# Float64 weight blocks assembled on other engines: two integer passes on VectorE instead of three, one more activation on ScalarE, no clamp on GpSimd, and a new instruction order

## The chip, the cores and the metric

One core of a Trainium2 chip runs the kernel. The metric is the device time of one execution in microseconds (us). The kernel before was timed in three runs: median 474.81 us, lowest 474.49, highest 475.64.

## The reference: what is computed

Three stages on batch 2, sequence 768, model width 512 (8 heads of 64):

```
attention:  q, k hashed to 6 sign bits by proj; a key is masked unless all 6 bits agree with the query's;
            softmax(q k^T / 8) v                                  -> x  (2, 768, 512)
experts:    4 experts of width 64: q,k,v = x @ wq[e], wk[e], wv[e]; causal softmax attention, @ wo[e];
            the two best experts by x @ w_gate, weighted by a softmax over their two logits
mix:        xk = mu_k*x + (1-mu_k)*x_prev,  xr likewise
            out = sigmoid(xr @ w_r) * (relu(xk @ w_k)**2 @ w_v)
```

The last three weight matrices, `w_k` (512x1024), `w_r` (512x512) and `w_v` (1024x512), reach the kernel as float64. All products are made with float16 pairs (a high part and the rest), three matmuls for one product, so each weight is needed as a float16 pair.

## The kernel before, in words

The program treats 12 blocks of 128 rows (6 for each batch). Each goes through attention (per head: scores `s`, exponential `P`, float16 pair `PHL`, transposed pair `PT`, product `x`), experts (`qk`, `vg`, `se`, `y`, `o`) and mix (`m32k`, `m32r`, `mk`, `mr`, `h`, `r`, `v`). Blocks overlap: while one is in its attention, earlier ones are in their experts or mix.

The weights are loaded and split once, in the first part of the run. `split_d` treats one 128x512 block of a float64 matrix; it is called 20 times (8 blocks of `w_k`, 4 of `w_r`, 8 of `w_v`). The block comes as pairs of 32-bit words (`raw`: word 1 `top` holds sign, exponent and high mantissa bits, word 0 `low` the rest). A float32 is put together bit by bit:

- ScalarE takes the absolute value of `top`, read as a float32, into `wm` (called `mag` in the code).
- GpSimd clamps `wm` from below and above, in place.
- VectorE, pass 1: shift `wm` left by 3 and mask, into the PSUM tile `wd`. Pass 2: OR in the upper three bits of `low`. Pass 3: OR in the top two bits of `top`.
- ScalarE writes the float16 high part of `wd` (tiles `WK`, `WR`, `WV`), and VectorE the rest ("the rest pass").

Engines named in the profile: PE is TensorE, DVE is VectorE, ACT is ScalarE, POOL is GpSimd, SP issues nearly all DMAs.

Every instruction is recorded first (class `Program`) and then issued in an order that is written out: `ORDER`, a packed list of indices, gives one sequence for all engines, and `HOMES` gives each tile its buffer. Each engine takes its instructions in that sequence. So an instruction that waits holds up all that stand behind it on its engine. All instructions are issued from one line (L200), so the profile tells them apart by tile names. Other passes that the prediction speaks of: `naq`, `nak` and `v` on VectorE (the rest passes of queries, keys and values; each subtracts one tile in SBUF from another tile in SBUF), and on GpSimd the rest pass `PHL<-P,PHL` of every softmax, which reads two tiles in SBUF.

Of the kernel before, what the change touches and what calls it, by code (L numbers as in the profile page):

```python
# [909 lines left out]
AL`%`NekJrE;Pr2xEcy!3(SFQ;11rywNMU|lBY$`5WB-9Ish49G9{yyco5b>D{O>?aWNc%eb5O5{SD<YIUR=17=eyJe!P#>aXL+<wpbVAQb%ZwZLkQYpiVFg  # L910
8sicuic_c}N2HPP6CH)6@BmZNC`d)iU>d!|hd6_l!z=s~X3}i>3*u2noDEH|7|wz9@B!OldyGnR;Wfsmc`%FSLo|AXkMRw5h9}qq7C-`eiwP+ab-+0^kDB5_
I18yMF?GSYG@rWSQ+$ryFgkt2?)VA+rti1`Ho`j`0>@xIJ;NCE8NXmJ?2W(UCU}8SXfyo40XPu1z##00G3gvUwD)+G7EljNPsiaa#-d0x1kb}z9ERWU8Ugjk
p12i|7ScB8gM*Q1KlR0*=>T1)3viHz;~yA@rr-#?2$L`}#U`e+l!25S4TTdRG!;+6IjY1N$><VH#>-HRtMDPZL8ss<ROVqY3e!*$s>*3;1^q|=z<F9kS70oT
!+#+it)vY!8mHlOJWONoH2j4#@D3cOOjMm~@CnLHH)%YM#JM;D&p<7%$=6^bU56Vm5wp-HnvK8lue_DAQcjwKwfR4&!}Bl)&BP;gi#F31I!cS_0v&TpXer%<
yKoEc!F-JBve7K;&)F##<)H<5lD5%8T!c@cE-$0sc{yFA+pvljV{Y0`tLYTohrILvrgC(*1efA6jOmu+eY!(`Vhr~X9zi{h<sQQt+ClZX0Y8PEv;r^DW%`Gr
xqs;yyn&MRC&hNZ&?=1U9#AP-jnjAoo~B*2mex@Px<^;2G?k$>IDpsVK>mw1VjQ;;<GH`_7(Isst}Hd=P52h}Qai3lmFWfSqlE4ywCDJ)95v!fG>F&YI=oA}
X%98$rrels(=a|m@1O-Y<Cgp$rgH~=NL8pRHQ`slID;L|<nmOFPPoBboj$;8$VVTcAU&c_Fpjt2W6Dp3=m`}j!6H<YQs8*rj$3gXeuiQ+frs-`QY=obxFhet
o!FXF;t(!ChP%+?2%g2Wxf6Hh67-C^a!sm5zfui)LC@(W1$;$sXd<V=Hr$PC({3EeqqsZ&MiH<My`@BMGcMqF)P=u5TTbj=(`Y{KhVpyr!GEyl)L553(r5ZY
&FCvd<TMx<xE>*=#c!0v)u*rU6Mv#~IG3kz8CTXZf2Z{LfyQu8p2XkaJ2aqP91$mTN|(VAN8m{8_y_goKAg%mq`o{<gp;}-(2oJLxh6D+Pr7-W+Ld$J-6_|I
# [33 lines left out]
HOMES = """
c-lQwi?-S}5S-c7TdKpQ;4~?v#)Rho|F9#ITmc7;ywc8V0p<$TK*mnji|&~bg!Y=}VsuN5aHz%uh7LGrZraeh;t#k5-0fd}vw!#nfAPuxF#Jz^<=^~ijvp$l
_Jz&9;lqCL%AY9sj>xafB&t_NFMQxb`>48*qeSgzdb4hb34)e{YBc7SvDt1D$a@JXtd?28<m#&@_kCNe-kK0EOqmPSxA4s*4zN^_4!R%7rV72HN`TNC6Edb2
$5I(2NH7;`cAtXuEql9N)c0f`D{jDpy0?0m!ewL*!E|vSNI(~;=n*9}(N2eQ#}YNSDZzoPOiIf&MPAw}?k~je6UCS?hBp~dDpF6hNOdYTzMBP4=&FkLaNTt*
kzuN4O%8gKbK=UoI`fh4H|}jk$C;&bH9n`WJ|s?1929^g-br{$i){TZ^}`;9-%Bc}ac7ws@LU5@kO{6rOV=0dazhg3lksYHIyiK+9?^UtTG2<uvy`<qq)d^t
i~UAVnL@O{QKh~ISLTNCVe;V7&I_NH2XB7!%Uv+I4QWrQ;3^cz_dAxPjE$0^fYEYelVBdKt4uekq>J2OL#t}6Q1mI3?L5xEiFR398|OiJd=)~wo}Mqew8bBG
rL8#4sxHu(Q|}y_Vl)^=bd)q7@aT}R>+~;z`hlRJE8;k!WxSuWS--qA4axTH>6=CoDWgc|(T&wAhN2*`n?f0ptN89G`-CeGtxqGNYq9Ryy081ywtmJ%qMlzD
#Z{6iWi^i@-rYMxEIR2OqsU6hc9PkjSZ%h>l#*5Msr7K?r-HSe^z{_!g?BD-<*uig;T(w}yYP1?W5%8<On19XY0vd@2By=fCCHySJ1%xz<GgH|jAh+VxZblR  # L960
S$jWi%9G%ZfZAkNDw+lTLnu=S^N&hdQd|Y+i1{y-r>`+ir8R95&gCUvo5s8Eud}b))w@0UKMxuncK
"""


# [40 lines left out]
```

## Time and profile before

| | before |
|---|---|
| median of the runs | 474.81 us |
| the profiled execution's own time | 473.49 us |
| its span, first to last instruction | 471.3 us |
| PE, DVE, ACT, POOL busy | 428.7, 354.1, 344.6, 320.8 us |
| mean granted TensorE clock | 0.978 of full speed |

Busy times are sums over the whole span; stages have different limits, so the rows further down are cut by stage. Times in rows are us unless they say ns. In rows of groups the columns are: line, engine, operation, output<-inputs, shapes, count | busy us, mean ns of one | idle time of the engine just before them and what ended it.

### The profile page before, as it was taken

What the parts mean: (1) busy time and instruction counts of PE and PEld (TensorE: products, weight loads), DVE (VectorE), ACT (ScalarE), POOL (GpSimd) and SP (SyncE); (2) the same over time, 40 slices, a digit from 0 to 9 for tenths busy, and PEclk for the clock granted to TensorE, in tenths of its full rate; (3) what the DMA queues carried; (4) which work ended last, traced back from release to release, by engine and by line L of the source; (5) the groups of instructions that cost most, each with busy time, mean ns of one, the idle gap of its engine ahead of it and who ended that gap; (6) DMA issues with size and microseconds to landing.
All of it is one profiled execution on the core that took longest, in us unless ns stands there. A gap on an engine that the chain in (4) does not pass through costs nothing.

```text
span 471.3 us, 15541 instructions
## 1 busy us (share of the span) xinstructions
PE 428.7 (91%) x6296; PEld 326.4 (69%) x6296; DVE 354.1 (75%) x990; ACT 344.6 (73%) x654; POOL 320.8 (68%) x321
## 2 busy tenths in 40 slices
PE   2873788788999999999999999999999999999996
PEld 2752476677667779687668768967857778787563
DVE  4999999999999887999776678675676634643422
ACT  4388897999999896659888987889678867353221
POOL 1878898788887958867888668669667753561010
PEclk9886999989999999999999999999999999999999
...
GB/s 256 273 236 167 196 187 212 152 184 196 188 193 197 155 184 170 170 161 166 188 205 168 159 148 175 171 131 202 166 151 102 169 160 24 113 96 56 76 69 45
DMA packets 227160, 75.59 MB, mean 160 GB/s; under 512 B 218512, under 2 KB 222736, under 8 KB 227088
## 3 DMA queue, kind: packets, MB, share of 16 engines
q1 hardware_dynamic: 225584, 74.48, 85.2%
...
## 4 chain that ended last, share of the span: by engine, by line
PE 59%; DVE 14%; POOL 12%; DMA 6%; issue 5%; ACT 2%; SPq 1%; ACTq 0%; POOLq 0%; DVEq 0%
PE v L200 12%; PE h L200 10%; PE s L200 7%; POOL PHL L200 7%; PE x L200 5%; PE r L200 5%; PE qk L200 5%; DVE P L200 3%; PE se L200 3%; PE y L200 2%; PE o L200 2%; PE vg L200 2%; PE tr_y L200 2%; DMA x<-nbq 2%; DVE wd_v L200 1%
## 5 line engine op out<-in xcount | busy, mean ns | idle before, releaser
L200 POOL TENSOR_TENSOR PHL<-P,PHL 128x768 f16<-128x768 f32 x96 | 158.9, 1666 | 30.6 <-ACT PHL L200 25.6
L200 DVE TENSOR_SCALAR_CACHE_REDUCE P<-s 128x768 f32<-128x768 f32 x96 | 91.1, 952 | 12.3 <-PE s L200 6.0
L200 ACT ACTIVATE P<-P,mx 128x768 f32<-128x768 f32 x96 | 89.0, 929 | 15.2 <-DVE mx L200 11.9
L200 PE MATMUL s<-y,x 128*128 128x384 f16 x384 | 80.5, 339 | 7.6 <-DVE P L200 5.1
L200 PE MATMUL h<-mk,WK 128*128 128x128 f16 x1152 | 74.1, 219 | 0.0
L200 PEld LDWEIGHTS <-WK 128*128 128x128 f16 x1152 | 67.6, 98 | 5.0 <-DVE vn L200 0.3
L200 PE MATMUL x<-v,PT 128*128 128x64 f16 x1728 | 63.4, 194 | 2.0 <-DVE g L200 0.8
L200 PEld LDWEIGHTS <-PT 128*128 128x128 f16 x1728 | 59.3, 99 | 7.8 <-DMA PT<-PHL 2.5
L200 ACT ACTIVATE PHL<-P 128x768 f16<-128x768 f32 x72 | 59.9, 838 | 5.0 <-DMA PT<-PHL 1.9
L200 PEld LDWEIGHTS <-x 128*128 128x128 f16 x576 | 41.2, 99 | 31.3 <-issue 11.1
L200 PE MATMUL v<-WV,k2h 128*128 128x512 f16 x192 | 57.1, 379 | 0.0
L200 POOL TENSOR_TENSOR PHL_m<-P_m,PHL_m 128x512 f16<-128x512 f32 (+2 forms) x24 | 33.8, 1424 | 19.2 <-ACT PHL_m L200 18.8
L200 PE MATMUL qk<-xT,WQK 128*128 128x128 f16 x576 | 37.1, 219 | 0.7 <-DVE xT L200 0.5
L200 PE MATMUL v<-WV,k2l 128*128 128x512 f16 x96 | 36.4, 379 | 0.0
L200 PEld LDWEIGHTS <-WQK 128*128 128x128 f16 x576 | 33.9, 98 | 3.1 <-issue 1.2
L200 PE MATMUL r<-WR,mr 128*128 128x512 f16 x144 | 35.7, 379 | 0.0
L200 DVE SCALAR_TENSOR_TENSOR h<-h,t 128x512 f32<-128x512 f32 x24 | 16.7, 696 | 21.5 <-ACT t L200 21.5
L200 ACT ACTIVATE P_m<-P_m,bias_m 128x512 f32<-128x512 f32 (+2 forms) x24 | 19.7, 820 | 14.0 <-DVE P_m L200 13.5
L200 POOL TENSOR_SCALAR PHL<-P 128x768 f16<-128x768 f32 x24 | 20.5, 853 | 10.7 <-ACT P L200 8.9
L200 ACT ACTIVATE t<-h 128x512 f32<-128x512 f32 x24 | 14.1, 589 | 18.0 <-PE h L200 18.0
L200 POOL TENSOR_TENSOR mk<-m32k,mk 128x512 f16<-128x512 f32 x12 | 13.9, 1158 | 18.2 <-ACT mk L200 18.2
L200 PEld LDWEIGHTS <-k2h 128*128 128x128 f16 x192 | 16.8, 98 | 12.3
(143 smaller groups left out, 877.7 us busy)
## 6 DMA issues: line engine op xcount, KB each, us to landing
...
PT<-PHL SPq DMA_TRANSPOSE x88, 4.3
```

The source lines that it names most:

```text
L200: getattr(getattr(self.nc, engine), method)(*[real(a) for a in args], **{k: real(a) for k, a in kw.items()})
```

## The change

`split_d` puts the float32 together in another way:

```diff
-F64_MIN = float(np.array([0x38100000], np.uint32).view(np.float32)[0])
+REBIAS = 2.0 ** -112
...
-        top, low = raw[:, :, 1], raw[:, :, 0]
-        nc.scalar.activation(mag, top.bitcast(F32), AF.Abs)
-        nc.gpsimd.tensor_scalar(mag, mag, 3e38, F64_MIN, op0=OP.min, op1=OP.max)
+        top = raw[:, :, 1]
+        end = sp.tile([P, n], U32, tag="b2", bufs=NB2, name=f"we_{nm}")
+        nc.scalar.activation(mag, top.bitcast(F32), AF.Abs, scale=REBIAS)
+        nc.scalar.activation(end, raw.bitcast(U8)[:, :, 3], AF.Copy, bias=-15.5 / 32, scale=1.0 / 32)
         w = dps(f"wd_{nm}", [P, n])
         u = w.bitcast(U32)
-        nc.vector.tensor_scalar(u, mag.bitcast(U32), 3, 0x3FFFFFFF, op0=OP.logical_shift_left, op1=OP.bitwise_and)
-        nc.vector.scalar_tensor_tensor(u, low, 29, u, op0=OP.logical_shift_right, op1=OP.bitwise_or)
-        nc.vector.scalar_tensor_tensor(u, top, 0xC0000000, u, op0=OP.bitwise_and, op1=OP.bitwise_or)
+        nc.vector.scalar_tensor_tensor(u, mag.bitcast(U32), 3, end, op0=OP.logical_shift_left, op1=OP.bitwise_or)
+        nc.vector.scalar_tensor_tensor(u, top, 0x80000000, u, op0=OP.bitwise_and, op1=OP.bitwise_or)
...
 ORDER = """
-(2566 entries, packed)
+(2546 entries, packed)
 HOMES = """
-(1291 entries, packed)
+(1311 entries, packed)
```

The absolute value is now multiplied by a power of two, so no mask and no clamp are needed. The upper three bits of `low` are made by ScalarE from the highest byte of `low` (times 1/32, with a bias so that rounding cuts off) into a new SBUF tile `we` (called `end` in the code). VectorE's new pass 1 reads two SBUF tiles, `wm` and `we`, and writes PSUM; its pass 2 puts in the sign.

`ORDER` and `HOMES` are new throughout. Read as instructions, the two orders compare so:

| | before | after |
|---|---|---|
| VectorE instructions | 810 | 790 |
| ScalarE instructions (without DMA issues) | 494 | 514 |
| GpSimd instructions | 317 | 297 |
| TensorE groups, SP's DMAs | 724, 215 | 724, 215 |
| assembling passes of VectorE ahead of `xT` of block 0, 1, 2, 3 in its queue | 21, 31, 42, 55 of 60 | 14, 20, 28, 37 of 40 |
| instructions of VectorE ahead of these | 116, 167, 236, 311 | 111, 156, 220, 296 |
| ScalarE instructions ahead of the last `P` of block 1, 2, 3, 4 | 70, 106, 145, 194 | 74, 115, 161, 210 |
| assembling passes of a block that stand directly behind one another | 2 pairs | 9 pairs |
| changes between exponential and sigmoid on ScalarE, the first included | 16 | 18 |

Among the instructions that both have, many stand elsewhere (by the longest common sequence 435 of TensorE's 724 groups, 441 of VectorE's 750, 96 of SP's 215), mostly by a few places. SP's first DMAs are before: queries, keys, a part of `wv`, and three more of keys; after: queries, the four of keys, then values.

## Rows read from the trace of the kernel before

**Rows 1.** The page: span, and busy time, share and instructions of each engine.
```profile
span 471.3 us, 15541 instructions
...
PE 428.7 (91%) x6296; PEld 326.4 (69%) x6296; DVE 354.1 (75%) x990; ACT 344.6 (73%) x654; POOL 320.8 (68%) x321
```
**Rows 2.** Busy time by stretch, us from the span's start.
```profile
core 0: us, PE busy (x) PEld busy (x) DVE busy (x) ACT busy (x) POOL busy (x), PEclk, DMA share, GB/s
0.00:12.00 12.00, 3.64 (x32) 3.22 (x33) 5.75 (x9) 5.82 (x7) 1.98 (x7) 1.00 0.90 255
12.00:96.00 84.00, 62.88 (x928) 48.06 (x927) 82.39 (x213) 65.13 (x124) 71.45 (x75) 0.90 0.93 203
96.00:160.00 64.00, 58.54 (x923) 46.26 (x919) 62.27 (x182) 61.73 (x122) 54.50 (x55) 0.97 1.02 188
12.00:160.00 148.00, 121.42 (x1845) 94.32 (x1843) 144.66 (x394) 126.86 (x245) 125.95 (x129) 0.93 0.97 196
160.00:460.00 300.00, 296.22 (x4382) 225.44 (x4381) 200.99 (x585) 210.05 (x401) 192.90 (x186) 1.00 0.84 143
460.00:471.30 11.30, 7.43 (x44) 3.43 (x41) 2.68 (x4) 1.82 (x3) 0.00 (x0) 1.00 0.12 46
```
**Rows 3.** The chain of waits, first us 12 to 160, then 160 to the end.
```profile
by line: POOL PHL L200 16.4%; issue 10.5%; DVE P L200 10.5%; PE qk L200 5.2%; DVE wd_v L200 4.4%; DVE wd_k L200 3.7%; DMA w_v<-in_moe_wv_dram 3.5%; PE s L200 3.4%; DVE x L200 3.2%; DVE y L200 2.4%; POOL PHL_m_p L200 2.3%; ACT P L200 2.0%; P
...
by line: PE v L200 17.4%; PE h L200 15.5%; PE s L200 9.3%; PE r L200 8.1%; PE x L200 7.8%; PE qk L200 5.2%; PE se L200 4.1%; PE vg L200 3.4%; PE y L200 3.4%; PE o L200 3.2%; DMA x<-nbq 3.1%; POOL PHL L200 3.0%; issue 2.0%; PE tr_y L200 1.7%
```
**Rows 4.** Timeline of DVE: start, length, operation.
```profile
74.48 0.69 DVE L200 TENSOR_SCALAR wd_r<-wm_r 128x512 uint32<-128x512 uint32 x1
75.08 0.15 DVE L200 TENSOR_SCALAR mx<-mx 128x1 f32<-128x1 f32 x1
...
151.87 0.69 DVE L200 TENSOR_SCALAR wd_v<-wm_v 128x512 uint32<-128x512 uint32 x1
152.60 1.42 DVE L200 SCALAR_TENSOR_TENSOR wd_v<-raw_v,wd_v 128x512 uint32<-128x512 uint32 x2
```
**Rows 5.** Tiles `raw_k` and `raw_v`: duration ns min/median/max, first and last start us.
```profile
L200 DVE SCALAR_TENSOR_TENSOR wd_k<-raw_k,wd_k x16: 681/689/697, 16.2 to 69.7; 128x512 uint32<-128x512 uint32 x16
...
L200 DVE SCALAR_TENSOR_TENSOR wd_v<-raw_v,wd_v x16: 674/696/709, 105.2 to 153.3; 128x512 uint32<-128x512 uint32 x16
L200 ACT ACTIVATE wm_v<-raw_v x8: 662/670/676, 100.1 to 148.6; 128x512 f32<-128x512 f32 x8
```
**Rows 6.** Tiles `naq` and `v` on DVE, as in rows 5.
```profile
L200 DVE SCALAR_TENSOR_TENSOR naq<-q,naq x12: 676/689/1546, 4.8 to 287.4; 128x512 f16<-128x512 f32 x12
...
L200 DVE SCALAR_TENSOR_TENSOR v<-v,v x8: 948/1418/2393, 25.2 to 230.3; 128x768 f16<-128x768 f32 x8
```
**Rows 7.** Busy time by stretch of tile `naq` alone, then of tile `v` alone.
```profile
core 0: us, PE busy (x) PEld busy (x) DVE busy (x) ACT busy (x), PEclk, DMA share, GB/s
12.00:160.00 148.00, 3.38 (x40) 2.62 (x40) 3.74 (x5) 4.35 (x7) 0.93 0.97 196
...
core 0: us, PE busy (x) DVE busy (x) ACT busy (x), PEclk, DMA share, GB/s
12.00:160.00 148.00, 30.26 (x672) 6.15 (x4) 3.35 (x4) 0.93 0.97 196
```
**Rows 8.** Timeline of POOL and DVE around 36 to 41 us.
```profile
36.28 3.96 POOL L200 TENSOR_TENSOR PHL<-P,PHL 128x768 f16<-128x768 f32 x2
...
37.09 3.96 DVE L200 SCALAR_TENSOR_TENSOR v<-v,v 128x768 f16<-128x768 f32 x2
```
**Rows 9.** Groups on POOL by costs, us 12 to 160.
```profile
L200 POOL TENSOR_TENSOR PHL<-P,PHL 128x768 f16<-128x768 f32 x41 | 68.1, 1670 | 9.5 <-ACT PHL L200 6.2 <-DVE wd_r L200 2.0 <-DVE P L200 0.4
...
L200 POOL TENSOR_SCALAR wm_v<-wm_v 128x512 f32<-128x512 f32 x8 | 4.9, 613 | 3.2 <-ACT wm_v L200 2.8
```
**Rows 10.** Timeline of ACT: start, length, operation.
```profile
105.05 0.68 ACT L200 ACTIVATE wm_v<-raw_v 128x512 f32<-128x512 f32 x1
105.61 0.51 ACT L200 ACTIVATE P_m_p<-P_m_p,bias_m 128x256 f32<-128x256 f32 x1
```
**Rows 11.** Groups on ACT by costs, whole span.
```profile
L200 ACT ACT_TABLE_LOAD x16 | 20.5, 1283 | 3.4 <-issue 2.5 <-PE r L200 0.6
```

More of the change, by code (lines that the diff above doesn't have):

```diff
@@ L14 @@
 U32 = mybir.dt.uint32
+U8 = mybir.dt.uint8
 BF16 = mybir.dt.bfloat16
@@ L910 @@
[L910 to L919, printed above, removed]
@@ new lines @@
+cL>V5k+2L>yXG+5r*Yl6wi^yd;BTzt4#O?o1a(|xm)2ErJzx}!fOPH`m(>00(m^u!o4e}LyQ6RnGPp>-o{Q|s*LROx6wiJ>tbpHLMi<p*a?9bd8|E9k>984|
+xPM$RSI*sVH(e9A5^lLwa2&)hgaz=_-FBJX2;abs@>N|!_tMpMBmD_j1f%_G$l~s}F}{(j=3cpReym>%YoMvy0%PF<MDu+iy1(lj+;bn?L_gmD>zcV|PW=-2
+!<i5MzI*QebX%dho8bR*ll*J<(Y0_t+%{MW58QV6<Q}>heg~ZOlYMK~#<g-0{0sNSfiH-kT|9rzpM<|%OBdHq@#p<p*WT@fw(b&qaToknUl`-~cCLeS{+)a8
+#=%!t2)Fs|eu(?#isBM~5q9|R4*f0|?nbzwZmIvvdEdwV<ceT1T;_jvm*EQZcYWPae;UTaazD(Sf~(Na4RA4iN7uzo^~d}fI19)9HQ4F9x$drq+vV@Ub%^Na
+`gy*mo9|=!;uzbn_VIlQEQtyHML*4thOX`$baDe-89Wbbd@nc0jdY{jAUE1w@`K$9pU@}rdwnVF?N<7KaSTj=vY6N>_sRS|Kf&$yo!weL-X--N@PvN=H{k{>
@@ new lines @@
+@b}?>ALqupF)oS!2X8@XybTlG9k}dQ`Q82vbi@%@4paE){-jUkC%L;Y*#Z5BQ`}Uy&d>0t{6lyI)7%fd=^agXGu%x77#8|j{<MDzDSanQ?VrF*H`~v0bNn8k
+#*f7ESOGiZdOzE3^x6FxzsMi-hx}Z(+}-l&eMX<jZ}9Wne7Df$@C#fnzsz0tSN&rD7AoR9*yPjtE?5Z{xx>Cb-tc>AiEDtHeP+MKcf}r91xMjh*AU-B7T*oi
+`TV|+{{THPgMS9kA*XMIxqWqC8MFFqez7~^ulQ@e27ZLmSQS4(HGBat;TMSJ#^6{i>{qxvzB=~8+rEG==vTWn&Qnc98i#lM09@sW?)rOv0y3?2O3m;U6!E{p
+Z!i#R;cE~wTIYIWZOrS7`iDNyBmcnP_rJp++~EFz7;e3*gHQdR@Yv_`#r!^Mj7_jRHph)F0u9FK?l1TZP4T&(j4NGTeBz(^7FgQ9@-f{fU)<-WufB|r<x2Qc
+zNG)`-}txwoqzAk`iNA{*TX*87hB>G{0c98Y}X3&P(S<|Ui+c=&Hv)d`wIRGeDTBarT^gbQXDr057K^WgKaS`9iXXrh<^1I{b4#nzx&qM4y*dgei*jLZ}1(w
@@ new lines @@
+`|khnk?1%76Z{MRz@PpnU&$w-iCD#t$De&tI!Y(#7{#OGbduuJ&yb9I@?SmyC8vB8jr!w%5S@NN44Q<S+-7%?GSe2f)m@^$eQ@Ba`N$NLwmEVM37vD(@T1R9
+QK$fIcmMiR^pD@={_{Wl4mTZZ`1-zq&q8&4L*K{){vRl2rJ5eGwy)*cU8Wg06UFUxyIm|wO?zBpzt`<^``rOYc+eekhh0=ENQ~+P1DZ1|OGjKHiiC+Nf{W-<
+P#Q{0J-9GsqCyk_6(hOG?lfJY*wn<Qq&U=7Qc)@$%2C`^dPY&*QTLo)P!TFhxo8&7#W{G)9e1;_6kVfqRM)4cY?PfMVm)7s7T`RLjInVc&c{WVfihAK%1Onk
+1ihqJ6c-m`ER2R{=q#P1*R%uIVhg_+oBC$HG&T28aVajt<rp2yQw55HQE&;Cq&IY)w%}GQLv4LKzYh1|PF#=saT~6{?RWrJ;woH?2XO=L!Zo-N|DbZz-dChv
++=n~(N^}S}VMo6kFXJBU&EKdp_2oaQA0NRR)YAV&Rj5B7#}nAv58#tHj9dA=c%8=a2(C+Qd;=QJH>nXdrV?@ttI}btPEDu=4dkPEf&Qj?lv*3oKh%_N(QW!p
@@ new lines @@
+r?45-r=RFwx<hyAKYB-lc@U4`Av~6=(I_6xr!fZBrZadJ@6mgzNwsJ^r%~Yh)X8`C7w{r}rSo_W-%@9fJdtDKNKU8c`4~^&pXn0*Lch`jx`Gd>4t=0|cnxph
+ReVHu@iyMU>)1^`(kE&`llgb*;-_#o-`(HDsr;BG@e}$?ztL0rLM`b6x1!_Rnx=6N-_u{@?s9^A`QE;d@9X>d{(gYJ#-6WpJNm$Hd7!_-)A=e7@@M%p-^cdU
+fjZMHp2@SBcm|*0bKH|0&*S+#hv#w^Vs1m1xFen7<}{8ja}PPmZK)IWqK|xof6#5d!@@WD7JuTd)SKRMH|j&(=@yQ&zO<1O;3n=ttNA`B#E1NtAMs{>z)yGy
+-{nNuQ<m};-pcWC8{gw)+*>~L7yio1|FZEnPK-(LJNJ^nePlcLr~mi|gY=^X{FE2+1B{P9@p4|li}+WLz|VLw|Hi-b02)Xsa0jQvh#Z+y;UG$ePQ3igYd9(X
+!BKc6Kj-(H98vz{zjzh@&FlCDujQQ_iTlca?kBsrzwG8{Jl+m)3{H)MDJl=4p%k58avI#j2RSw;W|2YihD`=YN>0LqB`zQ0beN7+e&Mt@P+oC7j?b?-0pHfW
@@ new lines @@
+oL=v07EaGe`7j^hn4FB`a4KHUu{cNuO~@HFIj7Zqe3Tc+5E&{Na2Tb>6~dAghtmieCL1_4XT+?W35Ux<StOY;3r3Jknu4=&8qUruB^!>S(ew|KWXBvBQJU)p
+i6mnvC$`X4(o!>UT290nITPpL%p6%p$ViDIqa`Qj!jTk1qDyWZBdv6`tdX^{SjI|g9Vcycl&q7&p{>T2yqu5oa~zo|xp*v%mpmL*qRB>?C7UFs#FE*PS#xP_
+o*<iLj%<;wGM*+=0iH%PD2q;_iIQ7i;w#L9ukj5|u<0~`=E_@~Cvjzo<i)JIO%g~VNh~FKsoc?cl1(R4eQlsKsi8K~Su{!B;beJ?PjJ0F!X1)C;>#3CDm!JD
+Jj4vLTn<SJd5;HWs!XA2GF>LwGMO*C<tZkVXP8Hy;|n|@$>bw`zymTv_DDv_EZH@+6bYFmjbxFmGMo0wJ~=8WC5L8{<nj&oOF=HgspJ!W$Dgn;f5x<uPO{5(
+xu*s7XDk}N;8*+w3+V&BuZN|u=8?S8So3N=ZKC-#y*$*MdQ6IFQ7xvwVhQ~Xi*k9bpv5?s<dob}QcGzOJ}x<=IG>P{@;iRld{Tl-YZ)z|O|`g|;<8*(D`{oT
@@ new lines @@
+FMnVat*T|Uy4KK|+DWVF87UyA<&;FTvr?LW(uy42VpuJ$tp(+RoRjlXNG?ieEyH!RoYvKt7R&xnux46V{?toyResiA)LA)xq(!Be6p_nvO^Qnu_V%k*;>!G&
+{;egYtaMSdf0XR0wAbr$Lt<O;5XWxH?=qEs(+YA$p2;nFA-AQYw$pmLiXQ6|T}>UdtCp6@Hq}bWU0FkOXeG_1`P5Bc%5!-ozw14zEDxl+_Rxwl#mYz}c_{bg
+kvvtlfAv3oEU)F6zLAM`N1kg{UP3SRmA=+D`c~iRQd&kIbRP9lv*omw7SK9cNQ-DOebi4n%~sH7{i3}!o+Y%NI#7G*6A^o_!Pe6T+HLP8uAR0Ivd8*sdG4zb
+Y=HLDDY}t1(MQ>95iOB@k|BD=rfOpQEK6;f#kY6zR@4URS^FY`b-I4lVOoK!$TxkVhb@u~*CRGmr|ArxsmpDJowLX`LPzRmDiKPCqc%!MYZM!!V|A9Ew+mK{
+_t}0c76$v-deNd<sW4u*&=1{gTWqV<;Cc2{zR3amF2^i^)#RUKEB!2MtQJ@2U*#7`V%sdKjnfG_-;!Aq-bUML2Q}mAw$^I%I@?Kgd4|oj-(;mt)a16^cGyl!
@@ new lines @@
+WhtyFueUl}PG;F`o1~L<m6Z<7Ikly<KcpW2B~C&AmLIafy#6D9$_7hk>Fv0sv9#8P+j0wT$#ZqSw&UD3N9XBfYsIa3p)JsbTF~;?B3q=3b&38fb8L;Cu+^5q
+GFl-kW~c0$owT{ORLfX#%WNBMu`SajcF^)#Su1BHti0s2^46Xkh7MexJ8}bV$c^}_^$7W`G4~9OLMF><*(|%|u*PAPuF&PWQnMH;=_V^_t2L)xw;NW<8d_;9
+U~9EQIApu56JN2;e91b7GNFky3AwDW6|o9d)VAwQD;qk6Th=)=4b4IgsV>{JTqqy9@NL_w8?;yG9r}bjRyov^DxtD9lZv)ZtJ+4bW?Qsss20|1HEArhLhVq+
+no5gMOKM9c8xSglilHmlk-E}1R1a09WvFg-LJeyb?pkxHX<b6sP|I4%eS2yxq?Np|)}c*!Wi`TUdt;SC^HAIJVYe_a3<__pZ8+g-hPt6%s2|#edsa{C%L998
+&+NIqw0HL28c0KFB#$k!M$xDmO&{448ytp&|D<1N5b9g|P|rSCYiT2GrJa1Uk5<R(TKDj)wU-XkQAUK}VN@6yHtA*^8is}M*1&$U==!()V>`5wjR|e+Uu$Nq
@@ L951 @@
+{{hr&8aD
 """
 HOMES = """
[L954 to L957, printed above, removed]
@@ L962 @@
+YZBEgBKx*M?)TdX%k?61Ry*JBb`#E{;yPu>0Lnbpl*g%&u1PV=$NBP=hVHI>OpRC3oAS_8V%8kCeWn`M{md2n)n%TIc9m)+F5>dg>mpDTF;<nTw!3b-eUZfR
+xQUkQAks_s&<yh-pSjoBZ_7G*j<a=p=rmC+-_-|VH3*>*5XLjXdQm4-E^GbjUaCEMPD9bCLlC%W=Fm#@wE6A)z;50D1v+aWO8
 """
```

54 lines of the change are left out of this document (15 added, 39 removed).

## The prediction

> **What bounds the kernel now.** I read the page first. TensorE is busy 428.7 of 471.3 us [rows 1], so at most some 42 us of the span are open to any change that leaves its matmuls alone, and this one does. The question is where those idle microseconds lie, so the next view is busy time by stretch [rows 2]. From 160 to 460 us TensorE is busy 296.22 of 300: there nothing but TensorE counts. In the last stretch it idles 3.9 us around the last output. Nearly all of the rest is early: 8.4 us before us 12 (the first loads), and 26.6 us of the 148 between 12 and 160. In that stretch VectorE is busy 144.66 of 148 us, 97.7%. ScalarE (126.86) and GpSimd (125.95) are near 86%. So TensorE waits there because VectorE can't hand it its operands faster.
>
> The chain of waits says the same with a reservation [rows 3]. From 160 on it runs through TensorE's own lines. From 12 to 160 it runs over VectorE passes (the assembling passes `wd_k` and `wd_v` among its longest items), but the largest single item is GpSimd's rest pass `PHL`, 16.4%. VectorE is the fullest engine, and GpSimd's softmax passes are threaded between its own. All 20 weight blocks lie in this stretch: their passes 2 and 3 start between 16.2 and 153.3 us [rows 5]. What the change saves on VectorE, it saves where VectorE sets the pace.
>
> From us 160 on TensorE needs the same work as before, so I take a microsecond gained before 160 to be a microsecond gained at the end. The queue counts in the section on the change allow it: ahead of `xT` of block 3 VectorE has 18 assembling passes fewer and 15 instructions fewer in all, so the new order does not put much else in their place. The sum is made on the profiled execution's stretches; its own time, 473.49 us, is 1.3 us under the median of 474.81, and I apply the difference to the median.
>
> **VectorE: what goes.** One of three assembling passes per block. Its length is 0.69 us [rows 4, 5], but successive independent instructions overlap: after a pass started at 74.48 the next instruction started at 75.08, 0.60 us later [rows 4]. The stretch's price is that spacing: 20 x 0.60 = 12.0 us.
>
> **VectorE: what comes.** Pass 2 of the new form is like the old passes, one SBUF input and PSUM, which never leave 674 to 709 ns [rows 5]; no change. Two things make it dearer than a plain deletion.
>
> First, passes that depend on one another and stand directly together can't overlap: passes started at 151.87 and 152.60, 0.73 apart instead of 0.60 [rows 4]. Such pairs go from 2 to 9: 7 x 0.13 = 0.9 us.
>
> Second, the new pass 1 has two inputs in SBUF. No assembling pass of before has that, but `naq` and `v` do, and they behave differently [rows 6]: `naq`, of the same 512 columns, takes 676 ns at best and 1546 at worst; `v`, of 768, takes 948 at best, 1418 in the median, 2393 at worst. The long ones meet GpSimd. At 37.09 two `v` passes take 3.96 us together instead of 1.9, while two GpSimd passes that began at 36.28 take 3.96 instead of 3.3 [rows 8, 9]: the four run by turns, and both engines lose. In the stretch 12 to 160 the five `naq` passes take 3.74 us (3.40 at the best length) and the four `v` passes 6.15 (3.80) [rows 7]: 2.7 us of waiting over 9 passes, 0.30 each. That is my price for the new pass 1, 20 x 0.30 = 6.0 us. The bounds are nothing (four of the five `naq` passes can hardly have waited) and 0.59 each, the mean of the four `v` passes: 0 to 11.7 us. The Trainium skill states this as a rule (page "SBUF — State Buffer", section "Who interferes with whom"): a VectorE instruction with two SBUF inputs contends with a GpSimd instruction that reads SBUF, and the one that comes second is blocked until the first has ended. The trace agrees at 37.09, and the page's rule is what speaks against this change; what it would cost if passes came at random moments is among the rivals.
>
> Together: 144.66 - 12.0 + 6.0 + 0.9 = 139.6 us of VectorE.
>
> **GpSimd.** It loses 20 clamps of 0.61 us [rows 9], 12.3 us, and gets back some part of the waits just counted, up to a pass length of 0.68 us when it comes second. With 125.95 us in 148 it isn't the fullest engine before, and less so after. I book no gain; the shorter path from load to pass 1 (one hop less) could help by fractions at the first blocks.
>
> **ScalarE.** It gets 20 activations of 128x512, with strided 8-bit input. No row shows that input; the nearest is `wm`, strided 32-bit, 0.67 us long [rows 5], with the next instruction 0.56 us after its start [rows 10]. 20 x 0.56 = 11.2; a form as slow as its full length would be 13.4. ScalarE's stretch goes from 126.86 to 138.1 us. That is the hidden price: VectorE at 139.6 and ScalarE at 138.1 are then equally full, and two in-order engines that feed each other don't both reach 97.7%. How far they get is to be read from 96 to 160, where both are full already: 62.27 and 61.73 of 64 us, the lower 96.5% [rows 2]. So the stretch needs 139.6 / 0.965 = 144.6 us instead of 148: 3.4 us gained.
>
> The two further table loads, 2 x 1.28 us [rows 11], fall after us 160, where ScalarE is busy 210 of 300 us [rows 2]; hidden by that idle time, 2.6 us if it were gone. The start (a new order of the key loads) I put at nothing, with 1 us either way; the tail has the same last matmuls and the same last pass.
>
> Forecast: 474.8 - 3.4 = **471.4 us**. Its own range: with waits between 0.2 and 0.4 us per pass the sum of VectorE moves by 2 us either way, so 469.3 to 473.4.
>
> **Rivals.**
>
> *No waits to speak of, ScalarE the limit.* If the new order puts pass 1 where GpSimd idles, as for four of the five `naq` passes, VectorE falls to 133.6 us. But ScalarE's 138.1 then sets the pace: at VectorE's former 97.7% the stretch is 141.3, 6.7 us gained, 468.1. If ScalarE were never idle, 9.6 us gained, 465.2; no lower than that. Against it: GpSimd is busy 85% of the stretch.
>
> *No change that can be measured.* The 8 blocks of `w_v` are assembled between 100 and 154 us, where ScalarE has only 2.3 us of idle time left in 64 [rows 2]. Their 8 x 0.56 = 4.5 us lengthen that part by at least 2.2 us, and by 4.6 at 96.5%; the other 12 blocks shorten 12 to 96 by 12 x (0.60 - 0.30) - 0.5 = 3.1 us. The result is 473.9 to 476.3. For it: ScalarE's count ahead of the last `P` of block 3 grows by 16, all of them new activations. Against it: ScalarE had room before 96 (65.13 of 84) to run ahead.
>
> *Slower, by the waits on GpSimd.* The place is the new pass 1, and with it all of VectorE's queue behind it. It decides from 0.46 us per pass: (144.66 - 12 + 0.9 + 20 x 0.46) / 0.965 = 148. With the `v` passes' mean of 0.59 VectorE has 145.3 us and the stretch 150.5: 477.3. A pass that comes at a random moment meets, by GpSimd's rows, 41 passes of 1.67 us and 57.9 us of shorter ones, 0.66 each on average [rows 2, 9]; half of the squares over 148 us is a mean wait of 0.52, so 476.1. For it: two `v` passes at 37 us. Against it: `naq`. By the page's rule named above nothing would shorten such a wait, since the pass holds or gets the read path for its whole length.
>
> That the change doesn't do what it says can't be: which instructions run on which engine is fixed. The order, new throughout, may by itself be better or worse by a microsecond or two; it is inside the range, and no row of before separates it.
>
> **How the numbers follow.** About 0.3%, 1.4 us, is what a measurement of this kernel can tell from no change: 473.4 to 476.2 counts as the same. The forecast gets 0.40, the first rival 0.17, the second 0.20 (of it 0.15 the same, 0.05 slower), the third 0.16 (its better end just the same: 0.03 of it), and 0.07 is left for the order, spread evenly. Faster: 0.40 + 0.17 + 0.02 = 0.59; same: 0.15 + 0.03 + 0.02 = 0.20; slower: 0.05 + 0.13 + 0.03 = 0.21. The range reaches from the first rival's floor to the third's price, 465 to 477.3.
>
> **What would show it.** By tile, the new pass 1 has a minimum near 0.68 us, a mean near 0.98 and single ones above 1.5, beside GpSimd passes that are longer than 1.67; pass 2 stays at 0.69. `we` takes 0.60 to 0.68 us. `wm` is gone from GpSimd. TensorE's total stays within 2 us of 428.7; its idle time falls by 3 to 4 us, all before 160. In the early stretch ScalarE and VectorE are both above 94%. The prediction is wrong if pass 1 never exceeds 0.7 us, if its mean is above 1.15, if `we` takes much longer than 0.68, or if TensorE's idle time after us 160 changes by more than 2 us: then the order, not the passes, made the difference.

## The result and the profile after

The kernel after takes 481.15 us (median of 4 runs, 479.14 to 481.72), the kernel before 474.65 us beside it (4 runs): ratio 1.0125, 95% interval 1.0093 to 1.0158. It is slower by 6.5 us. 471.4 was predicted, within 465 to 477.3: the time lies outside the range and the sign was wrong.

The profiled execution of the kernel after took 481.72 us. Its page, span and busy time:

```profile
span 479.8 us, 15530 instructions
...
PE 434.8 (91%) x6296; PEld 331.9 (69%) x6296; DVE 359.5 (75%) x970; ACT 358.1 (75%) x676; POOL 313.1 (65%) x301
```

Against [rows 1], VectorE is busy 5.4 us longer with 20 instructions fewer. TensorE has 6.1 us more for the same matmuls and idles 45.0 us instead of 42.6. Busy time by stretch (columns as in rows 2):

```profile
0.00:12.00 12.00, 3.32 (x26) 2.63 (x27) 4.42 (x6) 5.18 (x6) 4.97 (x11) 1.00 0.88 247
12.00:96.00 84.00, 65.28 (x877) 50.26 (x877) 79.92 (x195) 69.13 (x132) 60.39 (x59) 0.84 0.89 196
96.00:160.00 64.00, 54.74 (x843) 43.14 (x841) 62.23 (x165) 58.32 (x116) 46.89 (x42) 0.97 0.89 176
12.00:160.00 148.00, 120.02 (x1718) 93.40 (x1718) 142.15 (x359) 127.45 (x247) 107.28 (x100) 0.90 0.89 187
160.00:460.00 300.00, 295.55 (x4410) 225.98 (x4408) 208.29 (x600) 221.94 (x418) 199.70 (x191) 1.00 0.84 146
```

Beside [rows 2], TensorE has done 127 matmuls fewer between us 12 and 160 (1718 instead of 1845), and VectorE and ScalarE do more after 160: the work comes later. From 160 to 460 TensorE is as full as before. The assembling passes by tile, and then the busy time of the new pass 1 and of the new activation alone (tiles `we_k`, `we_r`, `we_v`; columns of the last three lines: DVE, ACT, clock, DMA):

```profile
L201 DVE SCALAR_TENSOR_TENSOR wd_k<-wm_k,we_k x8: 691/735/1890, 19.4 to 72.0; 128x512 uint32<-128x512 uint32 x8
...
L201 DVE SCALAR_TENSOR_TENSOR wd_v<-wm_v,we_v x8: 686/1352/2006, 111.5 to 161.8; 128x512 uint32<-128x512 uint32 x8
L201 DVE SCALAR_TENSOR_TENSOR wd_v<-raw_v,wd_v x8: 665/688/695, 114.3 to 162.5; 128x512 uint32<-128x512 uint32 x8
...
12.00:165.00 153.00, 8.67 (x8) 5.27 (x8) 0.90 0.89 186
...
12.00:165.00 153.00, 4.42 (x4) 2.59 (x4) 0.90 0.89 186
...
12.00:165.00 153.00, 10.28 (x8) 5.35 (x8) 0.90 0.89 186
```

The last assembling pass starts at 162.5 us; in [rows 5] it was 153.3. That is 9.2 us, and the span is 8.5 us longer: the loss is complete before the last block is assembled. The 20 passes 1 take 8.67 + 4.42 + 10.28 = 23.37 us; at their shortest, 0.69, it would be 13.8, so they wait 9.6 us, 0.48 each. One of them beside GpSimd, in the timeline:

```profile
111.28 1.64 POOL L201 TENSOR_TENSOR PHL<-P,PHL 128x768 f16<-128x768 f32 x1
...
111.48 2.01 DVE L201 SCALAR_TENSOR_TENSOR wd_v<-wm_v,we_v 128x512 uint32<-128x512 uint32 x1
```

GpSimd's pass ends at 112.92, and VectorE's, begun 0.20 us after it, ends 0.57 us after that: it stood still while GpSimd read.

Pass 1 is not the only one that waits longer. The groups of the `naq` passes, before and then after:

```profile
L200 DVE SCALAR_TENSOR_TENSOR naq<-q,naq 128x512 f16<-128x512 f32 x12 | 9.6, 801 | 4.8 <-ACT naq L200 4.8
L201 DVE SCALAR_TENSOR_TENSOR naq<-q,naq 128x512 f16<-128x512 f32 x12 | 14.2, 1184 | 0.0
```

The same 12 passes take 4.6 us more. In the experiments below they take 9.5 to 12.1 us in the old order, and 11.4 and 12.6 in the two runs of the new one. With the 9.6 us of pass 1 that is 14.2 us of waiting, about as much as the 20 passes that were left out (20 x 0.69 = 13.8 us).

### The profile page after: what moved, and what is told of

Read it like the earlier page. It is cut to its first block, busy times and chain, and to the rows that moved or that the text cites. A ratio compares the mean times of both kernels' runs of the same rounds, so it can differ in the third digit from the quotient of the medians.

```text
span 479.8 us, 15530 instructions
## 1 busy us (share of the span) xinstructions
PE 434.8 (91%) x6296; PEld 331.9 (69%) x6296; DVE 359.5 (75%) x970; ACT 358.1 (75%) x676; POOL 313.1 (65%) x301
## 4 chain that ended last, share of the span: by engine, by line
PE 44%; DVE 5%; DMA 3%; issue 1%; ACT 1%; SPq 0%; DVEq 0%; ACTq 0%
PE v L201 10%; PE h L201 9%; PE r L201 4%; PE x L201 4%; PE s L201 4%; PE qk L201 3%; PE se L201 3%; DMA PT<-PHL 2%; PE o L201 2%; PE y L201 2%; PE vg L201 2%; DVE P L201 2%; DMA x<-nbq 1%; DVE y L201 1%; DVE e L201 0%
## 5 line engine op out<-in xcount | busy, mean ns | idle before, releaser
L201 POOL TENSOR_TENSOR PHL<-P,PHL 128x768 f16<-128x768 f32 x96 | 161.1, 1687 | 44.3 <-ACT PHL L201 40.5
L201 PE MATMUL s<-y,x 128*128 128x384 f16 x384 | 82.7, 346 | 10.5 <-DVE P L201 8.3
L201 PE MATMUL x<-v,PT 128*128 128x64 f16 x1728 | 64.9, 196 | 2.5 <-DMA PT<-PHL 1.4
L201 PEld LDWEIGHTS <-PT 128*128 128x128 f16 x1728 | 60.5, 100 | 8.6 <-DMA PT<-PHL 2.6
L201 POOL TENSOR_TENSOR mk<-m32k,mk 128x512 f16<-128x512 f32 x12 | 14.4, 1200 | 24.1 <-ACT mk L201 23.9
```

What stands on the lines that cost most here:

```text
L201: getattr(getattr(self.nc, engine), method)(*[real(a) for a in args], **{k: real(a) for k, a in kw.items()})
```

## The experiments

In a diff `-` is the kernel that the edit starts from. "Old order" is the order of before with the added or removed instructions put in or taken out at their places; every ratio is against the kernel before on the same chip. The kernel before has medians from 474.5 to 475.27 us beside these runs, so between runs of different groups (e1 to e4, e5 to e8, e9 to e12, e13 to e16) the ratios compare better than the medians.

### Is it the new order, or the new split? (e1, e2)

e1 is the new `split_d` in the old order: the activation `we` stands where the clamp stood, pass 2 where pass 3 stood. e2 is the old `split_d` in the new order.

> The new split (two activations, pass 1 with two SBUF inputs, no clamp) in the old order: the new activation stands where the clamp stood, pass 2 is left out, everything else stands as before. Port theory (the waits of pass 1 on GpSimd eat what the removed pass saves): pass 1 means 1.0 to 1.3 us, and the time is within 3 us of before, 473 to 478. Order theory (the new order alone costs the 6.5 us): 466 to 471, since VectorE loses 12 us of passes in an order that is known to work. ScalarE theory: above 476, with pass 1 below 0.9 us.

Measured: 482.75 us, ratio 1.0147 (1.009 to 1.0203). No theory had both right: the mean of pass 1, 0.99 us, is just under the port theory's 1.0 to 1.3, but the time lies 4.75 us above its range. The 20 passes 1 (three lines, columns as for the kernel after) take 19.7 us, 0.30 of waiting each, as priced, and the last assembling pass starts as late as that of the kernel after:

```profile
12.00:165.00 153.00, 7.38 (x8) 5.18 (x8) 0.93 0.95 184
...
12.00:165.00 153.00, 4.47 (x4) 2.62 (x4) 0.93 0.95 184
...
12.00:165.00 153.00, 7.86 (x8) 5.37 (x8) 0.93 0.95 184
...
L201 DVE SCALAR_TENSOR_TENSOR wd_v<-raw_v,wd_v x8: 675/686/696, 114.4 to 162.6; 128x512 uint32<-128x512 uint32 x8
...
12.00:160.00 148.00, 117.94 (x1687) 91.29 (x1688) 135.04 (x355) 126.63 (x247) 107.68 (x99) 0.93 0.94 186
```

VectorE is busy only 135.04 of 148 us here, 9.6 less than before, and the kernel is slower all the same. So the loss needs no new order, and a full VectorE isn't what holds this kernel up. Whether the new order adds a loss of its own to the new split is not shown.

> The old split (three passes, clamp, one activation) in the new order: the clamp stands behind the later of the two activations, passes 1 and 2 stand together where the new pass 1 stood. Order theory: VectorE has 12 us more work and no waits of pass 1, so the time is above the changed kernel, 484 or more. Port theory: the 12 us of passes come back but some 10 us of waits go, so the time stays within 3 us of the changed kernel, 478 to 484.

Measured: 497.04 us, ratio 1.0448 (1.0405 to 1.0492). By its number it fits the order theory (484 or more). But the edit puts clamps and a third pass into an order that has no places made for them, so it tells little. Only this follows: the new order does not suit the old split.

### The waits of the new pass 1 (e3, e4)

e3 lets ScalarE write the low bits into the PSUM tile itself, in the new order, so that pass 1 has one input in SBUF:

```diff
-        end = sp.tile([P, n], U32, tag="b2", bufs=NB2, name=f"we_{nm}")
-        nc.scalar.activation(end, raw.bitcast(U8)[:, :, 3], AF.Copy, bias=-15.5 / 32, scale=1.0 / 32)
+        nc.scalar.activation(u, raw.bitcast(U8)[:, :, 3], AF.Copy, bias=-15.5 / 32, scale=1.0 / 32)
...
-        nc.vector.scalar_tensor_tensor(u, mag.bitcast(U32), 3, end, op0=OP.logical_shift_left, op1=OP.bitwise_or)
+        nc.vector.scalar_tensor_tensor(u, mag.bitcast(U32), 3, u, op0=OP.logical_shift_left, op1=OP.bitwise_or)
```

> The changed kernel, but the low bits are written by ScalarE into the PSUM tile, and pass 1 reads that and one SBUF tile. The activation moves back by up to 39 places where the PSUM buffer is not yet free. Port theory: pass 1 falls to 0.69 us each, VectorE gets some 9 us back, and the time falls to 471 to 475. Order or ScalarE theory: 478 to 482, no change that matters.

Measured: 483.93 us, ratio 1.0153 (1.01 to 1.0206), not the 471 to 475 of the port theory. The waits are gone, but others came. The pass by tile, then ScalarE's and VectorE's largest waits, us 12 to 160 (us in total, times, longest):

```profile
L201 DVE SCALAR_TENSOR_TENSOR wd_k<-wm_k,wd_k x8: 667/695/697, 19.8 to 72.6; 128x512 uint32<-128x512 uint32 x8
...
ACT wd_k L201 <- DVE y L201: 11.1, 2, 7.3
ACT wd_k L201 <- DVE WK L201: 3.7, 3, 2.4
...
DVE wd_v L201 <- ACT wd_v L201: 4.8, 7, 1.4
```

ScalarE now needs the PSUM buffer a whole step earlier and waits for its former users. The longest pass 1 falls from 1.89 us to 0.70: the second SBUF input is what made it wait. What the waits cost is not told by this run, since one wait took the place of another.

e4 adds the waits alone: the kernel before, whose pass 1 takes its mask from a tile in SBUF (32 columns, read again and again) instead of a constant.

```diff
-        nc.vector.tensor_scalar(u, mag.bitcast(U32), 3, 0x3FFFFFFF, op0=OP.logical_shift_left, op1=OP.bitwise_and)
+        nc.vector.scalar_tensor_tensor(u, mag.bitcast(U32), 3, masks, op0=OP.logical_shift_left, op1=OP.bitwise_and)
```

> The kernel before in its own order and with its three passes; only pass 1 takes its mask from an SBUF tile (32 columns, read over and over) instead of a constant, so that it has two SBUF inputs. Port theory: pass 1 means 0.9 to 1.3 us instead of 0.69, and the time rises by 3 to 9 us. If the waits are hidden: within 1.4 us of before.

Measured: 486.46 us, ratio 1.0235 (1.019 to 1.0279). The passes of the `w_v` blocks, the busy time of all 20 alone, then that of all engines:

```profile
L201 DVE SCALAR_TENSOR_TENSOR wd_v<-wm_v,masks x8: 697/952/2128, 111.8 to 164.2; 128x512 uint32<-128x512 uint32 x8
...
12.00:168.00 156.00, 23.28 (x20) 0.00 (x0) 0.90 0.86 182
...
12.00:160.00 148.00, 114.66 (x1675) 90.45 (x1675) 143.59 (x367) 116.06 (x223) 120.34 (x119) 0.90 0.86 185
```

The shortest of them take 0.70 us, so reading the same 32 columns again and again costs nothing by itself. 23.28 - 20 x 0.69 = 9.5 us of waiting cost 11.2 us (486.46 - 475.27), above the 3 to 9 that were expected. In this kernel, whose VectorE has no work taken away, the waits cost their full length and more.

### The new activations (e5)

The kernel before, with the 20 new activations made and not read:

```diff
+        end = sp.tile([P, n], U32, tag="b2", bufs=NB2, name=f"we_{nm}")
+        nc.scalar.activation(end, raw.bitcast(U8)[:, :, 3], AF.Copy, bias=-15.5 / 32, scale=1.0 / 32)
         nc.gpsimd.tensor_scalar(mag, mag, 3e38, F64_MIN, op0=OP.min, op1=OP.max)
```

> The kernel before, with the change's 20 new activations added where the clamps stand, their result unused. ScalarE theory (the added activations cost more than the 2 us that I booked): 479 to 486, about 0.3 to 0.6 us each. Port theory: ScalarE had the room, so within 2 us of before.

Measured: 477.86 us, ratio 1.0059 (1.0035 to 1.0082). From 96 to 160 us the activations fill ScalarE to 62.86 of 64:

```profile
96.00:160.00 64.00, 56.38 (x886) 44.73 (x885) 61.80 (x178) 62.86 (x124) 49.89 (x51) 0.97 0.96 179
```

About 3 us for 13 us of activations: less than the ScalarE theory's 479 to 486, more than the 2 us of the port theory. The profile shows no wait for a `we` tile or for its buffer, here or in e9, so the buffers that the new tiles take are not the reason.

### What the removed work was worth (e6, e7, e8)

e6 leaves pass 2 out of the kernel before (the second line here), e7 the clamp (the first line; the activation scales the bias away instead), e8 both. In e6 and e8 the lowest three mantissa bits of each weight stay zero.

```diff
-        nc.gpsimd.tensor_scalar(mag, mag, 3e38, F64_MIN, op0=OP.min, op1=OP.max)
-        nc.vector.scalar_tensor_tensor(u, low, 29, u, op0=OP.logical_shift_right, op1=OP.bitwise_or)
```

> The kernel before with pass 2 left out (so the lowest three mantissa bits of each weight stay zero), all else as before. It prices a VectorE pass in the old order. If VectorE sets the pace as I read it: 20 x 0.60 = 12 us less, 463 to 467. If a saved pass is worth only half because another engine follows: 468 to 471.

Measured: 473.36 us, ratio 0.9953 (0.993 to 0.9976): 2.2 us by the ratio, where 12.0 were taken off VectorE. The row by stretch, and the last assembling passes:

```profile
12.00:160.00 148.00, 122.26 (x1848) 96.29 (x1848) 135.96 (x373) 126.60 (x245) 127.06 (x129) 0.92 0.97 197
...
L200 DVE SCALAR_TENSOR_TENSOR wd_v<-raw_v,wd_v x8: 675/686/697, 106.6 to 153.0; 128x512 uint32<-128x512 uint32 x8
```

VectorE idles 12 us of the 148 instead of 3.3, and the last block is assembled at 153.0 instead of 153.3 us [rows 5]. The pass that was removed was real; the time it took was, but for those 2 us, not what the others waited for.

> The kernel before without the clamp (the scale takes the exponent bias away, three passes as before, the first with one SBUF input). If GpSimd is on the path as its share of the chain of waits says: 3 to 8 us less, 467 to 472. If not: within 1.4 us. If the clamp had kept GpSimd from running into the passes of the keys at the start: up to 2 us more.

Measured: 475.97 us, ratio 1.0012 (0.9988 to 1.0037). Leaving out the clamp is worth nothing in sum. Its first softmax pass comes 1.9 us later than before (see the start below), so what the freed 12 us of GpSimd are worth by themselves this run does not tell.

> Old order, no clamp, two passes, no new activation and no second SBUF input; the lowest three mantissa bits stay zero. It is the change without its two suspected costs. Port and ScalarE theories together: the removed work is worth what I booked or more, 460 to 467. If it stays at 472 or more, the gain was never there.

Measured: 475.07 us, ratio 0.9989 (0.9961 to 1.0018). Both savings of the change, without the new activations and the second input, give no gain in sum that can be measured. A late start is in this sum too: the first softmax pass comes at 23.6 us.

### Which resource holds the pace? (e9 to e13)

e9 puts the new activations, unread, on top of e8: the new split without its second SBUF input.

> The instructions of the new split in the old order, without its second SBUF input: no clamp, two passes on VectorE, the 20 new activations made but not read; the lowest three mantissa bits stay zero. Theory 'costs add up': two passes without the clamp gave 475.1 and the activations alone 2.8 to 3.1 us, so about 478; what is left up to the 482.75 of the new split in the old order, 4 to 5 us, is then the price of the waits on GpSimd (6.0 us of them there). Rival 'the activations fall into the gaps that VectorE now has': about 475. By the prediction's sum (VectorE 137.7, ScalarE 138) it would be 468 to 471.

Measured: 480.31 us, ratio 1.0121 (1.0091 to 1.015). Above e8 the activations cost 5.2 us by the medians, 6.3 by the ratios, whose intervals are far apart; 478 was expected if the costs add up. Us 96 to 160, the last passes of the `w_r` blocks and those of the `w_v` blocks, each time e8 and then e9:

```profile
96.00:160.00 64.00, 58.08 (x945) 45.92 (x942) 59.16 (x176) 62.26 (x124) 50.67 (x47) 1.00 0.99 190
96.00:160.00 64.00, 55.23 (x883) 43.39 (x882) 58.00 (x172) 61.97 (x123) 43.60 (x41) 1.00 0.93 177
...
L200 DVE SCALAR_TENSOR_TENSOR wd_r<-raw_r,wd_r x4: 677/682/686, 79.6 to 97.1; 128x512 uint32<-128x512 uint32 x4
L201 DVE SCALAR_TENSOR_TENSOR wd_r<-raw_r,wd_r x4: 674/682/690, 81.4 to 100.6; 128x512 uint32<-128x512 uint32 x4
...
L200 DVE SCALAR_TENSOR_TENSOR wd_v<-raw_v,wd_v x8: 672/686/697, 106.8 to 152.6; 128x512 uint32<-128x512 uint32 x8
L201 DVE SCALAR_TENSOR_TENSOR wd_v<-raw_v,wd_v x8: 673/690/707, 110.3 to 158.9; 128x512 uint32<-128x512 uint32 x8
```

From 96 to 160 us ScalarE is nearly full in both, VectorE in neither, and in e9 62 matmuls fewer get done. More than half of the delay is older: e9 is 3.5 us behind at the last block of `w_r` and 6.3 at the last of `w_v`.

Nothing in e9 waits on GpSimd in pass 1, and it is already as slow as the kernel after. The second input then adds 2.4 us between e9 and e1 by the medians, 1.2 by the ratios; their intervals overlap, so that part is not shown.

e10 reads the loaded words directly in pass 1, without absolute value and clamp; e11 leaves out one of the three passes as well; e12 loads only half of each block into the kernel before and uses it twice; e13 does that in e11.

```diff
-        nc.scalar.activation(mag, top.bitcast(F32), AF.Abs)
-        nc.gpsimd.tensor_scalar(mag, mag, 3e38, F64_MIN, op0=OP.min, op1=OP.max)
...
-        nc.vector.tensor_scalar(u, mag.bitcast(U32), 3, 0x3FFFFFFF, op0=OP.logical_shift_left, op1=OP.bitwise_and)
+        nc.vector.tensor_scalar(u, top, 3, 0x3FFFFFFF, op0=OP.logical_shift_left, op1=OP.bitwise_and)
```

and for the halved loads

```diff
-        LOADS.dma_start(raw.rearrange("p n a -> p (n a)"), src.bitcast(U32))
-        top, low = raw[:, :, 1], raw[:, :, 0]
+        LOADS.dma_start(raw.rearrange("p n a -> p (n a)"), src[:, :n // 2].bitcast(U32))
+        top, low = [raw[:, :, i].unsqueeze(1).to_broadcast([P, 2, n // 2]) for i in (1, 0)]
```

> Old order; the three passes read the loaded words directly, so ScalarE's absolute value (20 x 0.56 = 11.2 us) and GpSimd's clamp (12.3 us) are left out, VectorE's 60 passes stay (values outside the range of float32 would wrap). Theory 'ScalarE sets the pace together with others': it stood at 61.7 of 64 us in 96 to 160, so freeing it gives 2 us or more, 470 to 473. Theory 'no engine's fullness sets the pace, the loads or the chain through all do': within 1.5 us of before, 473.5 to 476.5. Theory 'VectorE alone sets the pace': no change either.

Measured: 476.0 us, ratio 1.004 (1.0016 to 1.0064). ScalarE and GpSimd, with 11 to 12 us of work less each, give nothing in sum either; that the kernel is 1.5 us slower goes with its late start (below).

> As the kernel without activation and clamp, and one of the three passes left out too (the lowest three mantissa bits stay zero): VectorE, ScalarE and GpSimd each lose 11 to 12 us of the 148 between 12 and 160. Theory 'two full engines have to be relieved together': 5 us or more gained, 469 or less. Theory 'the loads or the chain through softmax set the pace': no more than the 1.4 to 2.2 us of one pass less, 472.5 to 475.

Measured: 472.85 us, ratio 0.9965 (0.9943 to 0.9988). Three engines with 11 to 12 us less work each, and 1.7 us gained:

```profile
12.00:160.00 148.00, 124.38 (x1846) 97.06 (x1847) 137.46 (x374) 115.17 (x224) 112.21 (x106) 0.95 0.98 197
```

> The kernel before, but only the left half of each float64 block is loaded (256 KB instead of 512) and used twice, so half of each weight is wrong; all instructions of the engines keep their number and size. 5.2 MB less to move, at the 196 GB/s of the stretch 27 us of transfer time of 148. Theory 'the DMA engines, busy 97% from 12 to 160, set the pace': 5 us or more gained, under 470. Theory 'engines and chain, not the loads': within 1.5 us of before.

Measured: 475.1 us, ratio 1.0027 (1.0008 to 1.0046). The DMA share falls from 0.97 to 0.82 and nothing is gained:

```profile
12.00:160.00 148.00, 121.31 (x1841) 94.86 (x1840) 144.61 (x392) 126.02 (x244) 125.61 (x129) 0.95 0.82 163
```

> All engines relieved as in the kernel with two passes straight from the loaded words (472.85), and only the left half of each float64 block loaded and used twice (5.2 MB less; half of each weight is wrong). Theory 'the transposes through DMA, slowed by the weight loads, hold the pace once the engines are relieved': 3 us or more below 472.85. Rival 'the order of the queues and TensorE's own work hold it': 471.5 to 474.

Measured: 471.42 us, ratio 0.9926 (0.9902 to 0.995): 1.4 us under e11 by the medians, with intervals that overlap. The loads don't hold the pace either.

### The start (e14, e15, e16)

One thing is common to e7 to e11, e13 and e1, which have no clamp: their first softmax pass `P` starts at 23.4 to 24.1 us instead of 21.5. Its group (first and last start behind the lengths) in the kernel before, e11 and e14:

```profile
L200 DVE TENSOR_SCALAR_CACHE_REDUCE P<-s x96: 942/950/965, 21.5 to 373.2; 128x768 f32<-128x768 f32 x96
...
L200 DVE TENSOR_SCALAR_CACHE_REDUCE P<-s x96: 942/950/959, 23.5 to 374.0; 128x768 f32<-128x768 f32 x96
...
L200 DVE TENSOR_SCALAR_CACHE_REDUCE P<-s x96: 942/951/959, 21.4 to 369.9; 128x768 f32<-128x768 f32 x96
```

The clamp is not all that moves the start: e4 and e5, which have every clamp, start `P` at 22.7. What the missing clamp does, the timeline shows. VectorE's rest passes of the keys (`nak`) and GpSimd's work beside them; first the kernel before, then e11, then e14:

```profile
9.60 2.69 DVE L200 SCALAR_TENSOR_TENSOR nak<-k,nak 128x768 f16<-128x768 f32 x3
...
12.22 0.61 POOL L200 TENSOR_SCALAR wm_k<-wm_k 128x512 f32<-128x512 f32 x1 [6.22 <-ACT wm_k L200]
...
13.85 0.83 POOL L200 TENSOR_SCALAR nbk<-k 128x768 f16<-128x768 f32 x1
```
```profile
9.73 3.94 DVE L200 SCALAR_TENSOR_TENSOR nak<-k,nak 128x768 f16<-128x768 f32 x3
10.19 2.67 POOL L200 TENSOR_SCALAR nbk<-k 128x768 f16<-128x768 f32 x2 [3.38 <-DMA k<-in_k_dram]
```
```profile
9.48 2.69 DVE L200 SCALAR_TENSOR_TENSOR nak<-k,nak 128x768 f16<-128x768 f32 x3
...
12.10 0.62 POOL L200 TENSOR_SCALAR wm_k<-wm_k 128x512 f32<-128x512 f32 x1 [6.29 <-ACT wm_k L200]
```

In the kernel before, GpSimd stands for 6.2 us at the first clamp, which waits for the first block. Without the clamp it goes on to `nbk` at 10.19, reads the keys while VectorE's `nak` passes run, and these take 3.94 us instead of 2.69. The Trainium skill's rule (page "SBUF — State Buffer", section "Who interferes with whom"), which the prediction weighed for the new pass 1, fits here too, in instructions that the change doesn't touch: a VectorE instruction with two SBUF inputs contends with a GpSimd instruction that reads SBUF. The trace agrees on both sides: the two `nbk` passes take 2.67 us there, and 1.75 in the kernel before, where they come behind VectorE's.

e14 is e11 with the absolute value and the clamp kept for the first block; e15 is e10 with the same; e16 is e1 with one clamp, on the first block.

```diff
+        bits = top
+        if nm == "k21_0":
+            mag = sp.tile([P, n], F32, tag="b2", bufs=NB2, name=f"wm_{nm}")
+            nc.scalar.activation(mag, top.bitcast(F32), AF.Abs)
+            nc.gpsimd.tensor_scalar(mag, mag, 3e38, F64_MIN, op0=OP.min, op1=OP.max)
+            bits = mag.bitcast(U32)
```

> All engines relieved as above (472.85), but the first block keeps its absolute value and its clamp (lowest three mantissa bits zero throughout). Theory 'the clamp of the first block held GpSimd back from the keys' rest passes': those passes return from 1.58 to 0.95 us and the first softmax from 23.5 to about 21.5 us; if a late start is a late end, the time falls by 1.3 to 2 us to about 471. Rival 'the start's loss is made up before the first xT': no change at the end.

Measured: 470.82 us, ratio 0.9927 (0.99 to 0.9953). That is 2.0 us under e11 by the medians, though the intervals overlap. The passes are back at 2.69 us for three (above), and the last block is assembled at 149.5 us instead of 153.3:

```profile
L200 DVE SCALAR_TENSOR_TENSOR wd_v<-raw_v,wd_v x8: 675/686/695, 104.1 to 149.5; 128x512 uint32<-128x512 uint32 x8
```

> Three passes straight from the loaded words (476.0), the first block with its absolute value and clamp. By the start theory the first softmax returns to 21.5 us and the time to about 474; by its rival it stays at 476.

Measured: 474.04 us, ratio 0.9968 (0.9944 to 0.9992), against 1.004 (1.0016 to 1.0064) for e10: the intervals are apart. One clamp and one activation, put back, make the kernel 2 us faster by the medians, 3.4 by the ratios. The first softmax pass comes at 22.8 us, though, not at the 21.5 of the start theory. Against the kernel before, e15 is 1.5 us faster: so much 11 to 12 us less work on ScalarE and GpSimd each are worth once the start is nearly kept.

> The new split in the old order (482.75), with a clamp on GpSimd for the first block alone. By the start theory the first softmax comes at 21.5 instead of 23.9 us and the time falls by 1.5 to 2.4 us to about 480.8; what is left above 474.5 is then the activations (3 to 5 us) and the waits on GpSimd (2 to 3 us). By its rival it stays at 482.75.

Measured: 480.84 us, ratio 1.0137 (1.0097 to 1.0176). The median is where the theory put it, but the ratio hardly differs from e1's, the first softmax pass comes at 23.0 us instead of 21.5, and in the profiled execution the 20 passes 1 take 22.3 us, against 7.38 + 4.47 + 7.86 = 19.7 in e1. For the new split it stays undecided.

## Why the prediction was wrong

**The step that failed** is the premise: "TensorE waits there because VectorE can't hand it its operands faster", and with it the division of VectorE's sum by the fullness of its stretch. The row of 144.66 busy us in 148 was read as the pace. e6 takes 8.7 us out of that row and the end moves by 2.2; e11 takes 7 to 14 us out of three rows at once and it moves by 1.7; e14, with the start kept, by 3.5. So the 12.0 us of passes were worth about 2 in the old order. The reservation that the prediction read in the chain of waits [rows 3], GpSimd's `PHL` as its largest single item, was the better reading: VectorE did not hold the stretch by itself.

**ScalarE.** The length was right: 5.27 + 2.59 + 5.35 = 13.2 us, 0.66 each, within the 0.60 to 0.68 that were named (the sum had 0.56, from start to start). What was wrong is that VectorE's saving would pay for it. The activations cost 3 us alone (e5) and 5.2 us once VectorE has been relieved (e9 against e8). The rival "no change" had named ScalarE, in the 64 us from 96 to 160 where it had 2.3 us left. Its price, 2.2 to 4.6 us, was about the size of the whole cost, but the place was only half right: more than half of the delay is there before us 101 (e9 against e8), where ScalarE was said to have room, and the 3.1 us that were to pay for it there did not exist.

**The waits on GpSimd.** Direction and mechanism were right, the size in the new order was not: 0.48 us a pass instead of 0.30, just above the 0.46 from which the third rival was to decide, and near the 0.52 of chance arrival. The 4.6 us more of `naq` had no term at all. With exactly the 0.30 that was priced, e1 is no faster. So they are a part of the loss, not what turned its sign; alone they cost 11.2 us (e4), on top of e9 no more than a few.

**GpSimd** was booked at nothing, and in sum that is what e7 gives, with the loss at the start in it. **The start** was booked at nothing with 1 us either way. In the old order the missing clamp costs about 2 us (e15 against e10, and by the medians e14 against e11). The kernel after loses its start in another way: VectorE's first work is now a pass of the keys, for which it waits 6.4 us,

```profile
DVE nak L201 <- ACT nak L201: 6.4, 1, 6.4
```

where [rows 6] show the first pass of the queries at 4.8; the first softmax pass comes at 24.7 us, 3.2 later than before. No run prices this in the new order.

**The sum as the runs give it**, in the old order and by the ratios: one pass less -2.2 us (e6), without the clamp back to -0.5 (e8; that the start takes back most of it is argued, not shown), with the activations +5.8 (e9), with the second input +7.0 (e1; this last step is within the noise). The new order lies at +5.9, within the two kernels' spread. What was said to show it: minimum, singles and pass 2 came as forecast; the mean of pass 1, 1.17, is above the 1.15 that was named as wrong; TensorE's total rose by 6.1 us instead of staying within 2, and its idle time rose by 2.4 instead of falling by 3 to 4; ScalarE's stretch is 86% full instead of over 94; TensorE's idle time after 160 stayed, as forecast. The range ended at the third rival's price alone; that this, the activations and the start could come together was not in it. One figure of the first rival is a slip that changes nothing here: with ScalarE never idle, 148 - 138.1 is 9.9 us, not 9.6.

**What stays open** is what does hold the stretch from 12 to 160. Less work on VectorE (e6), on ScalarE and GpSimd (e15) or on all three (e14), or half the bytes of the weights (e12), gave 2.2, 1.5, 3.5 us and nothing; ScalarE alone was not tried. TensorE itself, busy 82% there [rows 2], and the latencies of a softmax threaded through four in-order queues and a DMA transpose are left; no run here separates these. The chain of waits of e11 from 12 to 160 points to the transposes, whose share in [rows 3] is not among those shown:

```profile
by line: DMA PT<-PHL 17.3%; PE s L200 11.3%; PE x L200 8.7%; issue 6.4%; DVE P L200 5.7%; PE qk L200 3.6%; PE tr_y L200 3.3%; PE v L200 3.1%; ACT P L200 2.9%; PE tr_x L200 2.9%; PE vg L200 2.7%; PE h L200 2.4%; DMA mur<-in_moe_mu_r_dram 2.3
```

All these prices hold for the old order, with work taken out of its places. What an order made for the lighter work would gain, no run tells; nor is it shown on which wait the activations' time is lost.
